# Attention with softcap, then a mixture of attention experts: the spare PSUM bank of the end section becomes a tile of its own

## Chip, cores and metric

One Trainium2 chip, one of its cores. The metric is the device time of one execution in microseconds (us), smaller is better; the time of a kernel is the median of its runs.

## The reference

Eight sequences of 448 tokens. First an attention with 12 heads of 64, whose scores pass through a soft cap of 30; then, on its output as 768 features, four attention experts of head size 64 with causal scores, of which each token uses the two that its gate ranks highest.

```python
scores = cap * np.tanh((q @ k.T) / sqrt(64) / cap)        # 8 x 12 heads, 448 x 448
attn = softmax(scores);  x = (attn @ v) as (8, 448, 768)

logits = x @ w_gate                                        # 4 experts, top 2 by logits
for e in range(4):
    qe, ke, ve = x @ wq[e], x @ wk[e], x @ wv[e]           # 768 -> 64
    a = softmax(causal(qe @ ke.T / 8))
    out += (e is chosen) * gate_weight * (a @ ve @ wo[e])  # 64 -> 768
```

## The kernel before

**The work.** The first attention goes in 48 steps, one for each pair of heads of a sequence. For a pair PE fills a score region in PSUM (L534), ACT takes the tanh out of it (L540, `y`), then the exponential of all seven blocks of the pair (L553; for the last pair in two halves, L548), PE multiplies with v (L565, L570), DVE divides (L581, L582, `xk`), and PE and DVE turn the result into `xT` (L592, L622). When the six pairs of a sequence are done, its experts follow, laid between the pairs of the next sequence: gate and v (L672), q and k (L794), expert scores (L813) and their exponential (L820, `pS`), the causal mask on POOL (L828), the product with v (L848, `pvS`), its scaling on DVE (L860, L862, L866, `o`), a sum on POOL (L874), transposes (L884, `otS`), their copy (L894, `oT`), the product with wo (L901), copies to SBUF (L916) and stores (L925).

**PSUM.** Its eight banks are divided by hand. `NAUX = 3` banks are single tiles of pool `ps_aux`, tags `aux0` to `aux2`. The other five are the score regions of pool `ps_score`, tags `sc0` with three banks and `sc1` with two (`CAPS = (8 - NAUX - 2, 2)`), which the tanh groups use in turn.

**The order.** The class `Sched` is a planner that runs while the program is being written: every piece of work has an engine, a duration, the pieces that it depends on and a due time, and the planner issues the pieces in the order of its own simulated clock. The order of each engine's list is thereby fixed (`manual_schedule`); the framework only adds the waits on semaphores, from which tile an instruction reads or writes. In the planner a bank is a number: 0 to 2 are the aux banks, and number 3 (`NAUX`) is the spare, which becomes free late, when the last tanh has read the three-bank region (`note_t` adds the piece `("spare",)`). A piece that takes bank 3 gets its tile from `spare()` instead of from `ps_aux` (in `Sched.aux`).

**The end section.** For the last sequence nothing is left to lay its experts between, so `add_last` has its own pieces (dictionary `L`). Once the last pair's tanh groups are done, the two score regions are taken as two end tiles (`l_tile`): one of three banks, and one of two. In the three-bank tile, banks 0 and 1 hold first q and k of experts 0 and 1 (L1036, copied to `qL`, `kL` by DVE and ACT, L1043), then the scores of one expert of each pair (L1111, read by ACT in L1117, `pL`), then an output block (L1186). The two-bank tile does the same for experts 2 and 3 and for the other expert of each pair. Bank 2 of the three-bank tile is the spare. Ten pieces pass through it in this execution, all of them named `end` in the profile because they share the tile: pvS of two windows (L848, read by L860 to L866), a pv of the last pair (L565, L570, read by L581, L582), v of two windows (L1050, read by ACT and DVE, L1075), a product with v (L1144, read by L1153 to L1160) and four output blocks (L901, read by L916). The masks of the last sequence are L1126, on POOL for experts 0 and 1 and on DVE for the others; the transposes and their copies are L1166 and L1176.

The order of PE's list from 288.7 us on is: q and k of feature block 4, pvS (spare), the gate, q and k of block 5 for experts 0 and 1, the same for 2 and 3, pvS (aux), v (spare, aux, spare), scores of experts 0 and 1, v (aux), v (spare, aux, spare, aux), pvS (aux), scores of 2 and 3, products with v (spare, aux), and then transposes and output blocks.

Of the kernel before, what the change touches and what calls it, by code (L numbers as in the profile page):

```python
# [9 lines left out]
f32 = mybir.dt.float32  # L10
# [230 lines left out]
def kernel(  # L241
# [37 lines left out]
    xp = ctx.enter_context(tc.tile_pool(name="xp", bufs=2))  # L279
    bp = ctx.enter_context(tc.tile_pool(name="bp", bufs=2))  # L280
    outp = ctx.enter_context(tc.tile_pool(name="outp", bufs=2))
    ps_score = ctx.enter_context(
        tc.tile_pool(name="ps_score", bufs=1, space=bass.MemoryType.PSUM)
    )
    ps_aux = ctx.enter_context(tc.tile_pool(name="ps_aux", bufs=1, space=bass.MemoryType.PSUM))
    CAPS = (8 - NAUX - 2, 2)

    ctx.enter_context(tc.manual_schedule())
# [223 lines left out]
    def group_of(i, cap):  # L512
        s = info[i]
        slots = []
        if s["rem"]:
            c = s["rem"].pop(0)
            slots = [(0, 0, c), (1, 1, c)]
        if s["tail"] and (not slots or (cap == 3 and s["reads"] > 0)):
            slots.append((len(slots), 0, KC))
            s["tail"] = False  # L520
        return slots, not s["rem"] and not s["tail"]

    def a_fill(p, slots, sc, tails):
        qt, kk = qkt[p]
        for at, g, c in slots:
            if (c == KC) != tails:
                continue
            o = sc[:, at, 0:S]
            r = slice(0, 128) if c == KC else slice(64 * g, 64 * g + 64)
            qs = qt[r, :]  # L530
            if p >= FIRST_Q:
                o = o.rearrange("p (m c t) -> p m c t", c=QC, t=16)
                qs = qs.rearrange("p (c m t) -> p m c t", c=QC, t=16)
            nc.tensor.matmul(o, kk[r, 128 * c : 128 * (c + 1)], qs, start=True, stop=True)  # L534
# [481 lines left out]
    L = {}  # L1016

    def l_tile(par):
        par = tail_par[par]
        if ("tile", par) not in L:  # L1020
            L["tile", par] = ps_score.tile(
                [128, CAPS[par], 512], f32, name=f"end{par}", tag=f"sc{par}"
            )
        return L["tile", par]

    def spare():
        x = [x for x in (1, 2) if tail_par[x] == 0][0]
        return l_tile(x)[:, 2, :]

    sch.spare = spare  # L1030

    def l_qk(r, which, j):
        if ("qk", r) not in L:
            L["qk", r] = l_tile(1 - r)
        w2 = wq2 if which == "q" else wk2
        nc.tensor.matmul(  # L1036
            L["qk", r][:, "qk".index(which), 0:S], w2[r][:, j, :], xT[LB][:, j, :],
            start=(j == 0), stop=(j == NDC - 1),
        )
# [64 lines left out]
    def l_fill(r):  # L1104
        ps = [L.setdefault(("s", r, g), l_tile(1 - g)) for g in range(2)]
        for c in (KC, 0, 1, 2):
            k0, q0 = (S - 128, KM) if c == KC else (128 * c, 128 * c)
            o = 0 if c == KC else SCOL[c]
            for g in range(2):
                rr = slice(64 * g, 64 * g + 64)  # L1110
                nc.tensor.matmul(  # L1111
                    ps[g].rearrange("p b c -> p (b c)")[:, o : o + S - q0],
                    kL[r][rr, k0 : k0 + 128], qL[r][rr, q0:S], start=True, stop=True,
                )
# [199 lines left out]
        nc.vector.memset(warm, 0.0)  # L1314

    def c_dummy():
        ps = ps_score.tile([128, CAPS[0], 512], f32, name="dummy", tag="sc0")
        for _ in range(7):
            nc.tensor.matmul(ps[:, 0, :], warm[:, 0:128], warm, start=True, stop=True)

# [70 lines left out]
    add(("warm",), "DVE", 0.27, [], -300.0, c_warm)  # L1391
    add(("ident",), "POOL", 0.6, [], -300.0, lambda: make_identity(nc, ident))
    add(("dummy",), "PE", 3.0, [("warm",)], -300.0, c_dummy)
    add(("table",), "ACT", 1.6, [("warm",), ("ld", "kt1", 0, "issued")], -300.0, c_table)
    for i in range(NST):
# [55 lines left out]
    def next_fill():  # L1451
# [14 lines left out]
        if ("trev", i) not in sch.done:  # L1466
            return None
        r = max(r, sch.done["trev", i][0] + 0.05)
        one = dict(r=r, dur=0.4, armed=armed, special=True, go=lambda s: go_t([i], s))
        if nf < 1 or not info[i]["rem"]:  # L1470
            return one
        nxt = pairs_of(i, 1)
        if nxt is None:
# [3 lines left out]
        two = dict(  # L1477
            r=max(r, r2), dur=0.75, armed=armed and armed2, special=True,
            go=lambda s: go_t([i, nxt[0]], s),
        )  # L1480
        if r2 <= max(r, sch.free["PE"]) + 0.05:
# [3 lines left out]
        return one  # L1485

    def tile_of(par):
        return ps_score.tile(
            [128, CAPS[par], 512], f32, name=f"sc_{state['nf']}", tag=f"sc{par}"
        )  # L1490

# [18 lines left out]
    def go_x(x, s, dur):  # L1510
        b, a = x
        sc = tile_of(state["nf"] % 2)
        s_fill(b, a, sc)
        state["x"].pop(0)
        key = ("X", b, a)
        dur += 0.1 if sch.mode == 64 else 0.0
        sch.mode = 128
        sch.free["PE"] = s + dur
        filled(key, s, dur)
        act_op(key, 0.905, [("f", *key)], lambda: s_exp(b, a, sc))  # L1520
# [4 lines left out]
    def go_t(which, s):  # L1525
        todo = []
        t = s + (0.1 if sch.mode == 128 else 0.0)
        for x, i in enumerate(which):
            par = (state["nf"] + x) % 2
            slots, last = group_of(i, CAPS[par])  # L1530
            sc = ps_score.tile(
                [128, CAPS[par], 512], f32, name=f"sc_{state['nf'] + x}", tag=f"sc{par}"
            )
            todo.append((i, slots, last, sc, par))
        ends = {}
        tails = 0.1
        for tail in (False, True):
            for x, (i, slots, last, sc, par) in enumerate(todo):
                a_fill(i, slots, sc, tail)
                k = sum(1 for at, g, c in slots if (c == KC) == tail)  # L1540
                if tail:
                    if k:
                        t += tails + S / 2400 + 0.003
                        tails = 0.0
                        ends[x] = t
                else:
                    t += k // 2 * (S / 2400 + 0.003)
                    ends[x] = t
        sch.mode = 64 if tails else 128
        sch.free["PE"] = t  # L1550
        for x, (i, slots, last, sc, par) in enumerate(todo):
            note_t(i, slots, last, sc, par, s, ends[x] - s)

    def note_t(i, slots, last, sc, par, s, dur):
        f = info[i]
        first, num = f["nb"], f["reads"]
        for at, g, c in slots:
            f["idx"][g, c] = first + at
        f["nb"] += len(slots)
        f["reads"] += 1  # L1560
        key = ("T", i, num)
        filled(key, s, dur)
        if i == NK - 1:
            tail_par[num] = par
            if par == 0 and num > 0:
                add(("spare",), "-", 0.0, [("T", i, num)], 0.0, lambda: None)
        adur = len(slots) * S / 1200 + 0.055
        act_op(key, adur, [("f", *key)], lambda: a_tanh(i, slots, sc, first))
        if num == 0 and i > 0:
            act_op(  # L1570
                ("E", i - 1), 7 * S / 1200 + 0.095, e_deps(i - 1), lambda: a_exp(i - 1)
            )
        if last:
            sch.finish(("filled", i), s + dur, "PE")
            state["piece"] += 1
            if i == NK - 1:
                for u, n in enumerate((WIN[2], S - WIN[2])):
                    act_op(
                        ("E", i, u), 7 * n / 1200 + 0.095, e_deps(i),
                        lambda u=u: a_exp_half(i, u),  # L1580
                    )
# [43 lines left out]
```

## Time and profile before

| | |
|---|---|
| median of 11 runs | 319.76 us (318.04 to 322.27) |
| the profiled execution | 318.04 us, of which the span of the profile is 316.0 |
| granted TensorE clock, mean | 0.971 |
| busy: PE matmul, PE weight load | 268.6 us (85%), 172.9 (55%) |
| busy: DVE, ACT, POOL | 203.4 (64%), 290.0 (92%), 177.1 (56%) |
| first matmul into an end tile | 282.74 us |
| end of the last exponential of the last pair | 286.44 us |
| last copy to SBUF starts (DVE) | 310.38 us |

Times within the profile count from the start of the span. A row of the timeline gives the start, the time from the start of its first to the end of its last instruction, the engine, the line of the kernel, the operation with what it writes and reads, and how many instructions it merges; in brackets stands the idle time of the engine just before it, and what ended it. A row of busy time by stretch gives for PE, PE weight load, DVE, ACT and POOL the busy time and the count of instructions, then the granted TensorE clock, the busy share of the 16 DMA engines, and the GB/s that they moved.

### The profile page before, as it was taken

The numbers are of one execution on the slowest core, as the hardware profiler recorded it, in microseconds if no ns is written. First come the engines' busy times: TensorE is split into PE (matmuls) and PEld (weight loads), VectorE is DVE, ScalarE is ACT, GpSimd is POOL, SyncE is SP. The second block draws the span as 40 slices with busy tenths as digits, with TensorE's granted clock in tenths as the row PEclk, the third lists the DMA queues.
The fourth block names the chain that finished last, engine by engine and source line by source line (L and its number), as shares of the span: only waits on it lengthen the run. The fifth ranks groups of instructions, "written<-read, shape, count | busy, mean of one in ns | idle before, by whom it ended". The sixth has DMA issues, their size and how long they took to land.

```text
span 316.0 us, 8056 instructions
## 1 busy us (share of the span) xinstructions
PE 268.6 (85%) x3073; PEld 172.9 (55%) x3073; DVE 203.4 (64%) x660; ACT 290.0 (92%) x229; POOL 177.1 (56%) x342
## 2 busy tenths in 40 slices
PE   6677678988899989998899899999899899987681
PEld 2344445665556755566555655755447565655550
DVE  3087435667477686757777566687576767654792
ACT  4889999999999999999999999999999999993541
POOL 6449690899419753678433993983439726230500
PEclk9579999999999999999999999999999999999997
DMA  5999999975988179943999186956899431020027
GB/s 161 266 230 210 235 205 158 212 188 142 227 229 206 37 193 199 308 101 86 205 282 228 23 220 151 259 152 192 225 235 250 97 99 52 2 75 2 0 95 256
DMA packets 93190, 52.87 MB, mean 167 GB/s; under 512 B 53792, under 2 KB 89760, under 8 KB 93152
## 3 DMA queue, kind: packets, MB, share of 16 engines
q1 hardware_dynamic: 81888, 50.19, 64.9%
q0 software_dynamic: 10512, 1.58, 7.2%
q10 hardware_dynamic: 752, 0.59, 0.8%
q8 instruction: 24, 0.39, 0.5%
q14 instruction: 14, 0.11, 0.1%
HBM read 36.19 MB, written 11.01 MB: 149 GB/s over the span
## 4 chain that ended last, share of the span: by engine, by line
ACT 64%; PE 19%; issue 6%; DVE 6%; POOL 3%; DVEq 0%; ACTq 0%; POOLq 0%
ACT pbuf L553 30%; ACT y L540 28%; ACT pS L820 4%; PE sc L534 3%; PE sc L813 2%; PE pv L570 2%; PE vps L672 1%; PE end L1036 1%; PE kps L794 1%; PE pv L565 1%; PE qps L794 1%; POOL ee L734 1%; PE wops L901 1%; DVE qs L803 1%; POOL mb L720 1%
## 5 line engine op out<-in xcount | busy, mean ns | idle before, releaser
L540 ACT ACTIVATE y<-sc 128x896 f16<-128x896 f32 x144 | 144.6, 1137 | 2.9 <-PE sc L534 2.9
L553 ACT ACTIVATE pbuf<-y 128x3136 f16<-128x3136 f16 x47 | 137.3, 2921 | 0.0
L534 PE MATMUL sc<-qk 64*128 64x448 f16 (+1 forms) x336 | 62.3, 367 | 11.6 <-ACT y L540 7.5
L570 PE MATMUL pv<-v,pbuf 128*128 128x65 f16 x1140 | 60.0, 194 | 0.0
L570 PEld LDWEIGHTS <-pbuf 128*128 128x128 f16 x1152 | 52.8, 98 | 4.8 <-issue 1.9
L565 PE MATMUL pv<-v,pbuf 128*128 128x130 f16 x190 | 42.8, 225 | 12.4 <-ACT pbuf L553 9.8
L534 PEld LDWEIGHTS <-qk 64*128 64x128 f16 (+1 forms) x336 | 20.3, 94 | 44.3 <-issue 36.8
L399 POOL CAST q<-qf 112x512 f16<-112x512 f32 x46 | 28.2, 615 | 26.3 <-DMA qf<-in_q_dram 26.0
L582 DVE TENSOR_TENSOR xk<-pv,rc 128x256 f16<-128x256 f32 x95 | 40.3, 425 | 3.3
L720 POOL COPY mb<-mk 128x1024 f16<-128x1024 f16 x14 | 14.2, 1039 | 45.2 <-DVE mk L715 45.2
L409 POOL CAST v<-vst 128x512 f16<-128x512 f32 x48 | 28.3, 619 | 7.4 <-DMA vst<-in_v_dram 7.4
L565 PEld LDWEIGHTS <-pbuf 128*128 128x128 f16 x192 | 18.8, 98 | 24.6 <-ACT pbuf L553 15.2
L581 DVE RECIPROCAL rc<-pv 128x4 f32<-128x4 f32 x95 | 16.9, 178 | 22.1 <-PE pv L570 21.6
L828 POOL TENSOR_TENSOR pS<-pS,keep 128x128 f16<-128x128 f16 (+1 forms) x56 | 21.0, 395 | 15.9 <-ACT pS L820 14.3
L622 DVE COPY xT<-xtp 128x448 f16<-128x448 f16 x48 | 18.5, 387 | 17.6 <-PE xtp L592 17.6
L916 DVE COPY ob<-wops 128x384 f32<-128x384 f32 (+1 forms) x48 | 25.5, 555 | 5.8 <-PE wops L901 5.2
L672 PE MATMUL vps<-wvg,xT 128*128 128x260 f16 x168 | 28.0, 275 | 0.0
L403 POOL CAST k<-kst 128x512 f16<-128x512 f32 x42 | 25.8, 616 | 0.1
L901 PE MATMUL wops<-wo,oT 128*128 128x384 f16 x112 | 24.9, 326 | 0.5 <-DVE o L866 0.2
L734 POOL TENSOR_TENSOR ee<-euler,lg 128x16 f32<-128x16 f32 x7 | 20.4, 2913 | 8.6 <-DVE lg L679 8.6
L794 PE MATMUL kps<-xT,wk 128*128 128x448 f16 x84 | 22.2, 352 | 0.9 <-DVE ob L916 0.4
L794 PE MATMUL qps<-xT,wq 128*128 128x448 f16 x84 | 22.3, 352 | 0.0
(171 smaller groups left out, 425.7 us busy)
## 6 DMA issues: line engine op xcount, KB each, us to landing
qf<-in_q_dram SPq DMA_DIRECT2D x22, 448.0 KB, 5.4
vst<-in_v_dram SPq DMA_DIRECT2D x23, 384.0 KB, 5.1
kst<-in_k_dram SPq DMA_DIRECT2D x22, 384.0 KB, 4.5
out_dram<-ob SPq DMA_DIRECT2D x18, 384.0 KB, 3.0
kst<-in_k_dram SPq DMA_DIRECT2D x47, 32.0 KB, 4.8
vst<-in_v_dram SPq DMA_DIRECT2D x47, 32.0 KB, 4.4
out_dram<-ob SPq DMA_DIRECT2D x6, 192.0 KB, 3.1
out_dram<-vst SPq DMA_DIRECT2D x3, 384.0 KB, 2.3
```

Of the source, the lines that this page charges most:

```text
L399: cp(c16["q", p], src.rearrange("p h (c d) -> p c h d", c=QC))
L403: cp(c16["k", p][:, 0:n], src.rearrange("p h c d -> p c h d")[:, 0:n])
L409: cp(v16[p % NV][:, :, :, 0:Dh], src)
L534: nc.tensor.matmul(o, kk[r, 128 * c : 128 * (c + 1)], qs, start=True, stop=True)
L540: nc.scalar.activation(ytile[i][:, first : first + nb, :], sc[:, 0:nb, 0:S], AF.Tanh, scale=isc / capf)
L553: nc.scalar.activation(ptile[i], ytile.pop(i), AF.Exp, scale=capf)
L565: nc.tensor.matmul(pv[:, n, :, :], ptile[i][:, idx[0, KC], w : w + 128], v16[i % NV][:, :, KC, :], start=(n == 0), stop=False, skip_group_ ...
L570: nc.tensor.matmul(pv[:, n, g, :], ptile[i][:, idx[g, c], w : w + 128], v16[i % NV][:, g, c, :], start=False, stop=(c == KC - 1), skip_gro ...
L582: nc.vector.tensor_tensor(xk, pv[:, :, :, 0:Dh], rc.broadcast_to((128, 2, 2, Dh)), ALU.mult)
L672: nc.tensor.matmul(ps, xT[b][:, j, w : w + 128], wvg[:, j, :], start=(j == 0), stop=(j == NDC - 1),)
L794: nc.tensor.matmul(s[which, r], w2[r][:, j, :], xT[b][:, j, :], start=(j == 0), stop=(j == NDC - 1),)
L901: nc.tensor.matmul(ps, s["oT"][:, r, w : w + 128], wo2[r][:, f * (D // 2) : (f + 1) * (D // 2)], start=(r == 0), stop=(r == 1),)
```

## The change

The pool `ps_score` becomes two pools, one for each region, so that each can be closed by itself. `ps_aux` is opened before them, and the regions lie at the two sides of what is left, so bank numbers change. At the end of the program the pool of a region is closed and a pool of the same size is opened in its place: with one two-bank tile, and, where the region had three banks, with a one-bank tile `spare` beside it. `spare()` hands out that tile instead of bank 2 of the end tile. The pieces, their order on each engine and their operands are as before.

```diff
-    ps_score = ctx.enter_context(
-        tc.tile_pool(name="ps_score", bufs=1, space=bass.MemoryType.PSUM)
-    )
     ps_aux = ctx.enter_context(tc.tile_pool(name="ps_aux", bufs=1, space=bass.MemoryType.PSUM))
+    sides = ("left", "right")
+    ps_ctx = [ctx.enter_context(ExitStack()) for _ in range(2)]
+    ps_score = [
+        ps_ctx[i].enter_context(
+            tc.tile_pool(
+                name=f"ps_score{i}", bufs=1, space=bass.MemoryType.PSUM, side=sides[i]
+            )
+        )
+        for i in range(2)
+    ]
...
     def l_tile(par):
         par = tail_par[par]
         if ("tile", par) not in L:
-            L["tile", par] = ps_score.tile(
-                [128, CAPS[par], 512], f32, name=f"end{par}", tag=f"sc{par}"
-            )
+            ps_ctx[par].close()
+            pool = ctx.enter_context(
+                tc.tile_pool(
+                    name=f"ps_end{par}", bufs=1, space=bass.MemoryType.PSUM, side=sides[par]
+                )
+            )
+            L["tile", par] = pool.tile([128, 2, 512], f32, name=f"end{par}", tag="end")
+            if par == 0:
+                L["spare"] = pool.tile([128, 512], f32, name="spare", tag="spare")
         return L["tile", par]
 
     def spare():
         x = [x for x in (1, 2) if tail_par[x] == 0][0]
-        return l_tile(x)[:, 2, :]
+        l_tile(x)
+        return L["spare"]
...
     def tile_of(par):
-        return ps_score.tile(
+        return ps_score[par].tile(
             [128, CAPS[par], 512], f32, name=f"sc_{state['nf']}", tag=f"sc{par}"
         )
```

The tiles of `c_dummy` and `go_t` are taken from `ps_score[0]` and `ps_score[par]` in the same way.

More of the change, by code (lines that the diff above doesn't have):

```diff
@@ L1316, in c_dummy @@
     def c_dummy():
-        ps = ps_score.tile([128, CAPS[0], 512], f32, name="dummy", tag="sc0")
+        ps = ps_score[0].tile([128, CAPS[0], 512], f32, name="dummy", tag="sc0")
         for _ in range(7):
@@ L1530, in go_t @@
             slots, last = group_of(i, CAPS[par])
-            sc = ps_score.tile(
+            sc = ps_score[par].tile(
                 [128, CAPS[par], 512], f32, name=f"sc_{state['nf'] + x}", tag=f"sc{par}"
```

## The prediction

> **What bounds the kernel now.** I read the page first, then the chain of waits, then the timeline from 281 us by engine, then busy time by stretch of the last 10 us. The page says where the change can act at all.
>
> ```profile
> span 316.0 us, 8056 instructions
> ACT  4889999999999999999999999999999999993541
> ```
>
> ScalarE is full for nine tenths of the span; the change touches nothing there. From slice 37 (284 us on) no engine is full: this is the end section, a chain through PE, DVE, ACT and POOL, and it alone uses the end tiles. The timeline shows what it waits for.
>
> ```profile
> 289.55 0.35 PE L1036 MATMUL end<-xT,wq 128*128 128x448 f16 x1
> 290.95 0.35 PE L1036 MATMUL end<-xT,wk 128*128 128x448 f16 x1 [1.06 <-DVE o L866]
> 292.58 0.49 PE L1050 MATMUL end<-wvg,xT 128*128 128x256 f16 x3 [0.40 <-DVE qL L1043]
> 292.91 0.49 PE L1050 MATMUL lv<-wvg,xT 128*128 128x256 f16 x3
> 295.65 0.49 PE L1050 MATMUL end<-wvg,xT 128*128 128x256 f16 x3 [0.95 <-ACT pL L1117]
> 299.44 0.34 PE L1144 MATMUL end<-vall,pL 128*128 128x65 f16 x6 [1.11 <-ACT pL L1117]
> ...
> 289.93 0.18 DVE L860 RECIPROCAL end<-end 128x2 f32<-128x2 f32 x1 [0.61 <-PE end L1036]
> 293.06 0.17 DVE L860 RECIPROCAL pvS<-pvS 128x2 f32<-128x2 f32 x1
> ...
> 294.30 0.37 ACT L1075 CAST vall<-end 128x256 f16<-128x256 f32 x1 [0.91 <-PE end L1111]
> ```
>
> In each row with a wait, one side works in banks 0 and 1 of the three-bank end tile (L1036, L1043, L1111, L1117) and the other in bank 2, the spare (L860, L866, L1050, L1075, L1144). No value passes between them. L860 needs what L848 wrote (289.11 to 289.61) and waits for a later q matmul; the k matmul needs xT (ready at 289.32) and waits for L866. So the order is kept per tile, not per bank. The two rows without a wait are the control: lv (292.91) and pvS are separate tiles of one pool, and PE writes lv while DVE is about to read pvS.
>
> Then what follows the compute.
>
> ```profile
> 306.00:308.00 2.00, 2.00 (x15) 1.20 (x13) 1.84 (x4) 1.18 (x3) 0.00 (x0) 1.00 0.88 346
> 308.00:309.00 1.00, 1.00 (x7) 0.47 (x5) 0.65 (x2) 0.66 (x2) 0.00 (x0) 1.00 1.01 399
> 312.00:313.00 1.00, 0.00 (x0) 0.00 (x0) 0.00 (x0) 0.00 (x0) 0.00 (x0) 0.50 0.97 252
> ```
>
> The last two columns are DMA share and GB/s: from about 306.2 to 314.1 the stores fill the DMA engines. The end therefore moves with the time at which the first stores come, not with the last DVE copy.
>
> **The change, part by part.** Nothing is added to any engine's list; no DMA is issued anew or moved. Each region is handed over once: the first matmul into it, at 282.74, already waits for the last tanh (0.17 us, from ACT L540), and should still do so. I cost the handover, the new bank numbers and the splitting of one score pool into two at 0; the trace has no row for them. What goes are the waits between the spare and banks 0/1. I follow the lists with the durations of the trace; handing over from engine to engine is 0.03 to 0.05 us there.
>
> 1. Before 286.5: the k matmul at 284.83 waited 0.51 for L866. Gain 0, because the pv matmuls at 286.49 wait for the exp half that ends at 286.44, and PE runs without a gap from there to 289.55.
> 2. The k matmul of 290.95 follows the q matmul by one step of 0.19: 289.74, 1.21 earlier. kL on ACT: 290.13 instead of 291.34. L860 starts at 289.64, after the last pvS matmul, so L866 ends at 290.62 and does not stand before qL. The qL copy still waits for kL (same tile, stays): 290.69. Second qL ends at 291.85 instead of 293.06: gain 1.21.
> 3. pvS moves to 290.31; lv into the spare needs only L866: 290.81 instead of 292.58 (1.77). Three groups of 0.33 fill PE to 291.79; the score matmuls L1111 need qL: about 291.9 instead of 293.66 (1.75).
> 4. ACT: vall no longer waits for L1111 and is done at about 292.5, when the scores are; pL starts at 292.5 instead of 294.57 (2.05). POOL's mask L1126 (3.23) runs 293.7 to 296.95 instead of 295.74 to 298.97 (2.0).
> 5. PE: the second lv into the spare no longer waits for pL: 292.8 instead of 295.65, and the second L1111 at 294.9 instead of 297.72 (2.8). That is more than the path can use, because POOL is now late next: the L1144 group needs the mask, 297.0 instead of 299.44, and POOL's L874 (1.15), which had waited for L866, stands right behind the mask at 296.97 instead of 299.05 (2.05).
> 6. From L874: otS 298.2, oT on ACT 298.85, then two lot copies behind it (0.80, 0.36, 0.36 apart), so the first L1186 at 300.4 instead of 302.50 (2.1). The L1186 group at 303.74 waited 0.30 for the vst copy out of the spare; that wait goes: 301.4 (2.35). The ACT copy of vst, 304.63 at present, follows: 302.3; on DVE the L1153 chain, which stood behind the vst copy, starts 2.45 earlier.
> 7. First stores therefore 2.35 to 2.45 earlier, and the full DMA stretch (7.9 us) moves as a whole. The last DVE copies lose two more waits (ACT kst at 309.32 is one) and end about 3.0 earlier, but hidden behind full DMA engines: 0 more.
>
> Sum: 2.4 us. The profiled execution took 318.04 (span 316.0 and 2.04 around it), so 315.6 with a span of 313.6. It is the fastest of the 11 runs; taking the same 2.4 from the median, 319.76, gives 317.4, a 0.75% gain. A measurement of this kernel tells about 0.5% (1.6 us) from no change.
>
> [...] In the trace wtokL (L1101) took 0.78 while POOL's L874 ran, where a product of the same shape with POOL idle (L1088) took 0.18. [...] With the change wunL and wtokL fall into POOL's mask (mask pieces of 0.42). [...] By the rows POOL's mask steps were evenly 0.38 apart and wunL beside a mask piece took 0.29: sum 2.4. I take the rows and keep 2.0 for the range.
>
> Bounds for what has no row. The handover: 0 if it waits as now; 0.1 if each region waits for both regions' last tanh (ending 283.49, 0.75 after the present one; the 0.51 wait that goes and the exp bound absorb most); above that see the third rival. Bank numbers: 0 either way, the granted clock of 1.00 and the durations of one shape agree across tiles now. If the stores do not bind after all, the gain is 3.0.
>
> **The rivals.** *Partial gain.* [...] Removing only the wait of 290.95 gives 1.0 to 1.2: 318.6.
>
> *No change.* The order might be kept by region or by pool, not by tile, so the split would remove nothing. Against: lv and pvS above. 319.8.
>
> *Slower.* Taking a new region may wait for more than the old region's own readers. If the matmul of 282.74 had to wait for ACT's list up to the last exp half (286.44), the PE work that now lies between 282.74 and 286.49 (3.75 less the 0.51 wait and small gaps of 0.2, so about 3.0) would come after it: 3.0 later at that point. The relief afterwards is 2.4 by the sum above, so 0.6 slower: 320.4. It decides from a handover ending at about 285.8; a loss over 1.6 us needs one up to 287.4, such as a wait for the last xk (288.21: 322.2). Against: the present row names ACT y L540 alone, and the old region's readers are only such tanh and exp reads.
>
> **How the numbers follow.** My forecast (1.8 to 3.0 gained) 0.74, partial 0.12, no change 0.07, slower 0.07. Within the forecast the case runs from 316.8 to 318.0; with about 0.3% for what a median moves between sets of runs (the 11 runs spread from 318.04 to 322.27), 316.2 to 318.5. The partial case reaches to 319.0 with it, so the range is 316.2 to 319.1; no change and slower are left out. Faster by over 0.5%: 0.74. Within 0.5%: the partial case, no change and half of slower with what noise adds, 0.21. Slower by over 0.5%: 0.05.
>
> **What would show it.** Right: the waits of L1036 on L866, of L1050 on qL and pL, of vall on L1111 and of L1144 on pL are gone; kL starts near 290.1, pL near 292.5, the mask near 293.7 and ends near 297, with L874 straight behind it; DMA is full from about 303.8 to 311.7. Wrong: the first matmul into a region starts clearly after 282.74; mask pieces over 0.42 us; DMA engines idle between stores.

## The result, and the profile after

| | before | after |
|---|---|---|
| median | 320.65 us (318.04 to 322.9, 50 runs) | 318.27 us (316.32 to 323.04, 13 runs) |
| ratio after / before | | 0.993, 95% interval 0.9908 to 0.9952 |
| profiled execution | 318.04 us, span 316.0 | 317.33 us, span 315.0 |
| last exponential of the last pair ends | 286.44 | 287.96 |
| from there to the end of the span ("the end") | 29.51 | 27.04 |

The change is faster by 0.7%, some 2.3 us. The two profiled executions differ by less, because everything up to the last exponential came 1.52 us later in the one of after. The profiled execution of before is the fastest of its 50 runs. The kernel below with new pools but no split has the main loop of after, and its runs take 0.9992 of the time of before (0.9969 to 1.0014). So the later start is put down to the execution, not to the change; in the ten other profiled kernels below, which all have that main loop, the last exponential ends anywhere from 287.25 to 293.32. All comparisons of profiles below therefore count from the end of the last exponential; to compare a row of after with one of before, take 1.52 off it. The lines of the kernel have moved by 7 to 14: L1050 was L1036, L1064 was L1050, L1125 was L1111, L1131 was L1117, L1140 was L1126, L1158 was L1144, L881 was L874, L891 was L884.

Two lines of the page of after; the second is ScalarE's busy share in 40 slices of the span.

```profile
span 315.0 us, 8054 instructions
ACT  4989999999999999999999999999999999995641
```

The same picture as before: ScalarE is full until the end section, and only there can anything have moved. These are the rows of the timeline of after that answer to those shown of before.

```profile
284.26 0.35 PE L1050 MATMUL end<-xT,wq 128*128 128x448 f16 x1 [0.17 <-ACT y L547]
...
291.07 0.35 PE L1050 MATMUL end<-xT,wq 128*128 128x448 f16 x1
291.26 0.35 PE L1050 MATMUL end<-xT,wk 128*128 128x448 f16 x1
292.33 0.49 PE L1064 MATMUL spare<-wvg,xT 128*128 128x256 f16 x3
294.29 0.49 PE L1064 MATMUL spare<-wvg,xT 128*128 128x256 f16 x3
296.90 0.20 PE L1158 MATMUL spare<-vall,pL 128*128 128x65 f16 x1
297.35 0.59 PE L1158 MATMUL spare<-vall,pL 128*128 128x65 f16 x5 [0.25 <-POOL pL L1140]
299.73 0.34 PE L891 MATMUL otS<-plain,o 128*128 128x128 f16 x3 [1.02 <-POOL o L881]
...
293.61 0.36 ACT L1089 CAST vall<-spare 128x256 f16<-128x256 f32 x1
294.05 1.94 ACT L1131 ACTIVATE pL<-end 128x1024 f16<-128x1024 f32 x2
...
295.21 3.23 POOL L1140 TENSOR_TENSOR pL<-pL,keep 128x128 f16<-128x128 f16 x8 [9.79 <-ACT pL L1131]
298.52 1.15 POOL L881 TENSOR_TENSOR o<-o 128x512 f16<-128x512 f16 x1
```

The k matmul follows its q matmul by 0.19; its wait of 1.06 for L866 is gone, and so are those of the v matmuls (0.40 and 0.95) and of the copy of `vall` (0.91). Where the products with v had waited 1.11 for ACT's reading of the end tile, they now wait 0.25 for POOL's mask, a real input. POOL's sum (L881) stands straight behind its mask and is what the transposes (L891) wait for: POOL is late next.

Busy time by stretch of after; the last three columns are granted TensorE clock, DMA share and GB/s.

```profile
304.00:305.00 1.00, 0.86 (x7) 0.52 (x7) 1.00 (x4) 0.22 (x2) 0.00 (x0) 1.00 0.00 0
305.00:306.00 1.00, 1.00 (x8) 0.59 (x6) 0.94 (x3) 0.67 (x2) 0.00 (x0) 1.00 0.97 387
312.00:313.00 1.00, 0.00 (x0) 0.00 (x0) 0.00 (x0) 0.00 (x0) 0.00 (x0) 0.90 1.01 326
313.00:314.00 1.00, 0.00 (x0) 0.00 (x0) 0.00 (x0) 0.00 (x0) 0.00 (x0) 0.50 0.19 74
```

The stores fill the DMA engines from 305.0 to about 313.2, for some 8 us as in before, and they begin and end earlier by about what the compute gained. (`vst` and `kst` are the SBUF tiles from which the last output blocks are stored; `otS` and `lot` are the transposed products of the last but one and of the last sequence, `oT` the copies of both.)

### The profile page after: what moved, and what is told of

Read it like the earlier page. It is cut to its first block, busy times and chain, and to the rows that moved or that the text cites. A ratio compares the mean times of both kernels' runs of the same rounds, so it can differ in the third digit from the quotient of the medians.

```text
span 315.0 us, 8054 instructions
## 1 busy us (share of the span) xinstructions
PE 271.2 (86%) x3073; PEld 174.6 (55%) x3073; DVE 203.1 (64%) x660; ACT 290.3 (92%) x229; POOL 177.1 (56%) x342
## 4 chain that ended last, share of the span: by engine, by line
ACT 60%; PE 19%; DMA 6%; issue 6%; DVE 4%; POOL 4%; POOLq 0%; ACTq 0%; DVEq 0%; SPq 0%
ACT pbuf L560 27%; ACT y L547 27%; ACT pS L827 5%; PE sc L541 4%; DMA qf<-in_q_dram 3%; DMA kst<-in_k_dram 2%; PE pv L577 2%; PE sc L820 2%; PE pv L572 1%; PE vps L679 1%; PE kps L801 1%; PE end L1050 1%; POOL ee L741 1%; PE wops L908 1%; PE qps L801 1%
## 5 line engine op out<-in xcount | busy, mean ns | idle before, releaser
L547 ACT ACTIVATE y<-sc 128x896 f16<-128x896 f32 x144 | 143.9, 1120 | 3.7 <-PE sc L541 3.7
L541 PE MATMUL sc<-qk 64*128 64x448 f16 (+1 forms) x336 | 63.7, 375 | 10.6 <-ACT y L547 6.8
L577 PE MATMUL pv<-v,pbuf 128*128 128x65 f16 x1140 | 60.9, 196 | 0.0
L577 PEld LDWEIGHTS <-pbuf 128*128 128x128 f16 x1152 | 53.8, 99 | 5.2 <-issue 2.4
L727 POOL COPY mb<-mk 128x1024 f16<-128x1024 f16 x14 | 14.2, 1039 | 45.0 <-DVE mk L722 45.0
L572 PEld LDWEIGHTS <-pbuf 128*128 128x128 f16 x192 | 19.1, 99 | 21.8 <-ACT pbuf L560 11.6
```

Of the source, the lines that this page charges most:

```text
L547: nc.scalar.activation(ytile[i][:, first : first + nb, :], sc[:, 0:nb, 0:S], AF.Tanh, scale=isc / capf)
L572: nc.tensor.matmul(pv[:, n, :, :], ptile[i][:, idx[0, KC], w : w + 128], v16[i % NV][:, :, KC, :], start=(n == 0), stop=False, skip_group_ ...
L577: nc.tensor.matmul(pv[:, n, g, :], ptile[i][:, idx[g, c], w : w + 128], v16[i % NV][:, g, c, :], start=False, stop=(c == KC - 1), skip_gro ...
```

## The experiments

Times are us after the end of the last exponential, from one profiled execution of each kernel; "end" is the end of the span. The theory was that the gain is the sum of what each removed wait costs at its place, and that new pools, new bank numbers and the handover of a region bring and cost nothing. The rivals: the pools or the banks themselves are the gain; a wait is worth more or less than its place says; or something later than the waits sets the end.

| kernel | k copy (kL) | pL | mask | transposes (otS) | first store | last DVE copy | end |
|---|---|---|---|---|---|---|---|
| before | 4.90 | 8.13 | 9.31 | 13.82 | 18.70 | 23.94 | 29.51 |
| after | 3.69 | 6.09 | 7.25 | 11.76 | 16.22 | 20.84 | 27.04 |
| new pools, not split | 4.91 | 8.14 | 9.31 | 13.82 | 18.69 | 23.93 | 29.54 |
| last two waits back | 3.69 | 6.09 | 7.25 | 11.76 | 16.22 | 21.44 | 27.06 |
| first two waits back | 4.92 | 7.32 | 8.49 | 13.00 | 18.61 | 22.85 | 29.20 |
| the same, again | 4.92 | 7.32 | 8.49 | 13.00 | 18.71 | 22.94 | 29.32 |
| the same, with filling | 4.92 | 7.32 | 8.49 | 13.01 | 17.46 | 22.07 | 28.38 |
| middle three waits back | 3.69 | 6.94 | 8.12 | 12.63 | 18.63 | 23.07 | 29.38 |
| the same, again | 3.69 | 6.94 | 8.12 | 12.62 | 18.57 | 22.81 | 29.14 |
| the same, with filling | 3.69 | 6.95 | 8.12 | 12.64 | 17.22 | 22.14 | 28.34 |

**New pools without the split.** The regions are closed and opened anew as in after, but the three-bank region is one tile again and the spare its bank 2.

```diff
-            L["tile", par] = pool.tile([128, 2, 512], f32, name=f"end{par}", tag="end")
-            if par == 0:
-                L["spare"] = pool.tile([128, 512], f32, name="spare", tag="spare")
+            L["tile", par] = pool.tile([128, CAPS[par], 512], f32, name=f"end{par}", tag="end")
...
-        l_tile(x)
-        return L["spare"]
+        return l_tile(x)[:, 2, :]
```

> The pools are closed and opened as in the changed kernel, with the new bank numbers, but the three-bank region is one tile again and the spare is its bank 2. Measure: time from the end of the last exponential half of the last pair to the end of the span, 29.6 us before (286.44 to 316.0), 27.0 in the changed kernel (287.96 to 315.0). Theory (the order is kept per tile, the split is the whole gain, the handover costs nothing): 29.6 again, all six waits between spare and end back, ratio to before 0.998 to 1.002. Rival (the handover or the other banks bring the gain): 27.0, ratio 0.993. Rival (the handover itself costs and the split gains more than it seems): over 29.8.

Measured: ratio to before 0.9992 (0.9969 to 1.0014), end 29.54, every step within 0.01 to 0.03 of before. Its timeline has the four waits of PE again, to the hundredth:

```profile
294.22 0.35 PE L1047 MATMUL end<-xT,wk 128*128 128x448 f16 x1 [1.06 <-DVE o L873]
295.85 0.49 PE L1061 MATMUL end<-wvg,xT 128*128 128x256 f16 x3 [0.40 <-DVE qL L1054]
298.92 0.49 PE L1061 MATMUL end<-wvg,xT 128*128 128x256 f16 x3 [0.95 <-ACT pL L1128]
302.71 0.34 PE L1155 MATMUL end<-vall,pL 128*128 128x65 f16 x6 [1.11 <-ACT pL L1128]
```

So the handover and the bank numbers are worth nothing that shows (0.03 us of the end), and the split is the whole of the gain. It also settles the slower rival: that mechanism would show here as a loss with nothing beside it.

**The last two waits put back.** The copy of an output block out of the end tile waits again for a later output matmul into the spare, and the copy out of the spare for a copy out of the end tile (`after` adds such an order between two instructions).

```diff
+        if (b, n, f) == (LB, 3, 0):
+            after(i, ("wo", LB - 1, 2, 0))
+        if (b, n, f) == (LB - 1, 2, 0):
+            after(i, ("ev", LB, 3, 1))
```

> The changed kernel with two of the old waits of the last copies put back: the kst copy of the last rows waits for the output matmul into the spare, the vst copy out of the spare waits for the ACT kst copy. Theory (the stores fill the DMA engines and set the end): the last DVE copy starts 0.6 later against the exp end, the span end does not move (27.0, within 0.15). Rival (the last copies set the end): 27.6.

Measured: the last DVE copy 0.60 later, the end 27.06 against 27.04. The waits that the change takes from the last copies are worth nothing: the DMA engines cover them, full with a busy share of 1.01 from 309.79 to 313.20 here.

**The first two waits put back.** The k matmul waits again for L873 out of the spare, and L867 of that window for the last q matmul.

```diff
+        if (b, n) == (LB - 1, 1):
+            after(i, "wq")
...
+        if (r, which, j) == (0, "k", NDC - 1):
+            after(i, ("o", LB - 1, 1))
```

> The changed kernel with two of the old waits put back: the k matmul of the last feature block waits for L873 reading the spare, and L867 before it waits for the q matmul. Theory (steps add up along one chain): the k matmul comes 1.2 us later against the exp end, the second score fill and the mask follow, and the exp end to span end takes 28.2 (27.0 plus 1.2). Rival (everything hangs on this first wait): 29.5. Rival (POOL's mask or the stores set the end anyway): 27.0 to 27.3.

Measured: kL, mask and the transposes 1.23 to 1.24 later, as expected, but the end at 29.20: 2.16 lost instead of 1.2. Up to the transposes the theory holds; behind them another 1 us goes that no wait accounts for.

**The middle three waits put back.** The first v matmul into the spare waits for qL, the copy of `vall` for the score matmuls, the second v matmul into the spare for the first pL.

```diff
+            if (n, j) == (0, 0):
+                after(m, ("q", 0))
+            if (n, j) == (2, 0):
+                after(m, ("x", 0, 0))
...
+            if n == 0:
+                after(i, ("f", 0))
```

> The changed kernel with three of the old waits put back: v into the spare waits for the first qL copy, the vall copy waits for the first score fill, the third v group waits for the first pL. Theory: the fill comes 0.4 later, the second fill 1.5 later, of which POOL's mask path hides 0.3; exp end to span end 28.2 (27.0 plus 1.2). Rival (everything hangs on the first wait): 27.0. Rival (each wait counts by its own idle time, 0.40, 0.91 and 0.95): 29.3.

Measured: mask and transposes 0.87 later, the end at 29.38: again 2.34 lost where 1.2 was expected. Either group alone put back thus takes away nearly the whole gain, which two separate costs cannot do. The busy time by stretch shows what the extra is, in a column that I had not counted with: the granted clock stands at 0.50 for 3.4 us, from 14.1 us after the last exponential in the first kernel and from 14.9 in the second. In before and after it is 1.00 from there to the last matmul.

**Both again, with runs for a ratio.** The mean granted clock differs from run to run (0.945 to 0.987 over the 55 runs of before beside these two), so both kernels ran once more.

> The two first waits put back once more (the k matmul behind the softmax work on the spare bank, and the first sum of sequence 6 behind the last q matmul), because in the first look TensorE's granted clock was 0.50 for some 3 us of the end and its length could not be used. Theory (every put-back wait moves the whole end by what it costs at its place): mask start 8.49 us after the last exponential (7.25 in the changed kernel), first sum of the last sequence otherwise as there, first store 17.45, end 28.2 us after the last exponential where the clock holds 1.00; ratio to the kernel before 0.997. Rival (the slow stretch belongs to the put-back wait): the clock is at 0.50 again at the same place, and the end comes at 29.2.

> The three middle waits put back once more, for the same reason. Theory: mask start 8.12 us after the last exponential, second filling of the spare bank 10.11, first store 17.1 to 17.45, end 27.9 to 28.2 where the clock holds 1.00; ratio to the kernel before 0.996 to 0.997. Rival (the slow stretch belongs to the waits): the clock at 0.50 again, end at 29.4.

Measured: ratios 1.0004 (0.9981 to 1.0028) and 1.0000 (0.9970 to 1.0031), ends 29.32 and 29.14, the clock at 0.50 again from 14.2 on in both. Three rows of the second of them, in the columns of the stretches above:

```profile
302.00:303.00 1.00, 1.00 (x6) 0.36 (x4) 0.92 (x6) 0.34 (x2) 0.00 (x0) 0.50 0.00 0
303.00:304.00 1.00, 1.00 (x17) 0.83 (x16) 0.76 (x3) 0.00 (x0) 0.00 (x0) 0.50 0.00 0
304.00:305.00 1.00, 1.00 (x13) 0.65 (x10) 0.89 (x5) 0.00 (x0) 0.00 (x0) 0.50 0.03 8
```

PE is full there. Two of the 384-column output matmuls (302.55) take 0.84 us from start to end, and 0.50 in after. So it is no chance: all four profiles of these two kernels show it, and their other runs lose the whole gain too.

**The waits put back, and PE kept at work.** In the four profiles with the fall PE has matmuls under way for only 1.67 to 2.06 us of the 3.41 before it, and waits there for POOL's sum (1.03 in the second profile with the first two waits back, 1.02 in both with the middle three). My guess was that too little work is the cause; then work without use in that wait must cure it:

```diff
         ps = sch.aux(("oT", b), [128, 2, 512], f16, f"otS_{b}")
+        if b == LB - 1:
+            for _ in range(14):
+                nc.tensor.transpose(ps[:, 0, 0:128], plain, plain)
```

> The two first waits put back, and 14 more 128-column transposes of a constant on TensorE ahead of the last sequence-6 transposes, into the tile that these overwrite: about 0.8 us of TensorE work that lies in its wait for the sum of that sequence. Theory (the half clock of the two earlier profiles comes from too little TensorE work in the stretch before it, not from the waits as such): granted clock 1.00 through the end, transposes at 13.0 us after the last exponential as without the filling, first store 17.45, end 28.2 to 28.3; ratio to the kernel before 0.996. Rival (the clock has another cause): 0.50 again at about 14.2 after the last exponential, end 29.2 to 29.3, ratio 1.000.

> The three middle waits put back, with the same filling. Theory: granted clock 1.00 through the end, transposes at 12.6 us after the last exponential, first store 17.1 to 17.3, end 27.9 to 28.2; ratio to the kernel before 0.995 to 0.996. Rival: 0.50 again from 14.1 to 14.9 on, end 29.1 to 29.4, ratio 1.000.

Measured: ends 28.38 and 28.34, each about 0.1 above the range expected, ratios 0.9964 (0.9936 to 0.9991) and 0.9959 (0.9927 to 0.9990). Against the ratios without filling the intervals still overlap a little, so the weight lies on the profiles, one of each kernel. Two rows of the timeline and one stretch of the first of them:

```profile
299.64 0.95 PE L893 MATMUL otS<-plain 128*128 128x128 f16 x14
300.84 0.34 PE L896 MATMUL otS<-plain,o 128*128 128x128 f16 x3 [0.24 <-POOL o L883]
```

```profile
303.00:304.00 1.00, 1.00 (x23) 0.87 (x24) 0.78 (x3) 0.00 (x0) 0.00 (x0) 1.00 0.00 0
```

The filling lies in the wait for L883, of which 0.24 is left, and the transposes start where they did. The clock stays at 1.00 up to the last matmul, and 0.94 and 0.80 us of the end come back, counted from the second profiles without filling. Now the waits cost what lies at their place: the first two 28.38 - 27.04 = 1.34, the middle three 1.30. Their sum, 2.64, is near the whole gain of 2.47.

**One sum moved from POOL to DVE.** Since POOL is late next, its sum for the last but one sequence is taken by VectorE right behind the last product of that sequence (in `s_pvev`); and in a second kernel POOL, free then, takes the mask of expert 2.

```diff
+        s["no"] = s.get("no", 0) + 1
+        if b == LB - 1 and s["no"] == 4:
+            o = s["o"]
+            nc.vector.tensor_tensor(
+                o[:, :, 1:5:3, :], o[:, :, 1:4:2, :], o[:, :, 2:5:2, :], ALU.add
+            )
...
     def s_oa(b):
+        if b == LB - 1:
+            return
```

The second kernel has this line besides:

```diff
-            (nc.vector if r else nc.gpsimd).tensor_tensor(
+            (nc.vector if 2 * r + g == 3 else nc.gpsimd).tensor_tensor(
```

> The changed kernel with the one sum of sequence 6 that stands between its products and its transposes (GpSimd, 1.15 us behind a 3.23 us mask) taken by VectorE right after the last product. Theory (with the waits gone GpSimd's mask and sum set the path to the transposes): the transposes start about 1.0 us earlier than 11.76 after the last exponential, VectorE's chain behind them is later by 0.3 to 0.45, the first output product starts 0.5 earlier, the end comes at 26.5 (27.04 in the changed kernel); ratio to the kernel before 0.9915. Rival (VectorE is itself full there, 293.4 to 301.3 without a gap, and takes back what GpSimd gives): the end at 27.0 or later, ratio 0.993 or above.

> The same, and the mask of expert 2 (0.72 us of VectorE) taken by GpSimd, which has nothing else to do there. Theory: the first output product as in the version with the sum alone, the second group of products over the last sequence is not held up by VectorE, end at 26.4; ratio to the kernel before 0.991. Rival (two SBUF inputs on VectorE beside GpSimd slow each other): small VectorE rows of 0.16 us stretch to 0.3 or more, end at 26.8 or later.

Measured: the sum alone gives 317.49 us, ratio 0.9904 (0.9868 to 0.9939), end 26.81; with the mask moved as well 317.92 us, 0.9919 (0.9897 to 0.9941), end 26.94. The first is the fastest of all kernels here by median and by end, but its interval overlaps that of after. From the timeline of the first:

```profile
295.39 3.42 POOL L1148 TENSOR_TENSOR pL<-pL,keep 128x128 f16<-128x128 f16 x8 [9.78 <-ACT pL L1139]
...
297.64 0.50 DVE L881 TENSOR_TENSOR o<-o 128x512 f16<-128x512 f16 x1
298.90 0.17 DVE L1123 TENSOR_TENSOR wtokL<-wunL,rdenL 128x16 f32<-128x16 f32 x1
...
299.89 0.28 PE L1188 MATMUL lot<-plain,oscL 128*128 128x128 f16 x2 [0.38 <-DVE oscL L1182]
300.65 0.23 PE L1188 MATMUL lot<-plain,oscL 128*128 128x128 f16 x1 [0.47 <-DVE oscL L1182]
```

The transposes start at 10.77 instead of 11.76, and the first output matmul at 12.64 instead of 13.38. But PE now waits for `oscL`, the products of the last sequence that DVE scales, and DVE, which has no gap there, comes to the output copies later: the first store gains 0.66, the second only 0.36, and the end 0.23 of the 0.5 expected. The rival of a full DVE holds for half. In the second kernel the end of 26.4 did not come either: as its rival said, the row of `wtokL` stretched (to 0.44, against 0.17 with POOL idle), the first output matmul came 0.26 after that of the first kernel, and the end is at 26.94.

## Why the prediction was right

**The map.** The forecast was a gain of 0.75%, 317.4 us, within 316.2 to 319.1; 0.7% and 318.27 came. Over 50 runs the median of before is 320.65, 0.89 above the 319.76 of 11 runs on which the forecast stood, which is the 0.87 that the figure in us missed by. The margin for that was thinner than stated: the range goes 0.5 to 0.6 us beyond the forecast's 316.8 to 318.0, while the 0.3% named for it would be almost 1 us. The times of the working, moved by the 1.52 of this execution, against the rows of after:

| step | forecast | after |
|---|---|---|
| 1 first matmul into an end tile waits as before | 0.17 for L540 | 0.17 for L547 |
| 2 k matmul; kL | 291.26; 291.65 | 291.26; 291.65 |
| 3 v into the spare; scores | 292.33; 293.4 | 292.33; 293.40 |
| 4 pL; mask | 294.0; 295.2 | 294.05; 295.21 |
| 5 second v into the spare; second scores; sum L881 | 294.3; 296.4; 298.5 | 294.29; 296.36; 298.52 |
| 6 transposes; oT; last-sequence output group; vst copy | 299.7; 300.4; 302.9; 303.8 | 299.73; 300.38; 302.78; 303.68 |
| 7 first store; last DVE copy; end | -2.35 to -2.45; -3.0; -2.4 | -2.48; -3.10; -2.47 |

The rows of the table hold to 0.15 us. That the 2.4 was not the sum of the removed waits (1.06 + 0.40 + 0.95 + 1.11 alone is 3.5) came from step 5, where POOL takes over as what is late, and from step 7, where full DMA engines cover the rest. The last-two-waits run shows step 7, and POOL's row (L881, 1.02 of PE's wait) step 5. Two terms were off. The `lot` copies behind `oT` took 0.60 for both, where the 0.73 of before was counted, and steps 6 and 7 came 0.1 earlier for it. And the products with v were put at 297.0 (298.5 here), behind the whole mask, but the first started at 296.90 and the rest from 297.35 on, each when the mask pieces that it needs were done. That moved nothing, since the sum on POOL ends later.

**DVE beside POOL.** The range kept a gain of 2.0 beside the 2.4 of the rows, 0.4 less for DVE and POOL slowing each other. No run shows that term; 2.47 came. DVE rows that are longer beside POOL are there, but they are small; the first two are of before, the third is of after:

```profile
299.05 1.15 POOL L874 TENSOR_TENSOR o<-o 128x512 f16<-128x512 f16 x1
299.45 0.78 DVE L1101 TENSOR_TENSOR wtokL<-wunL,rdenL 128x16 f32<-128x16 f32 x1
...
298.16 0.32 DVE L1115 TENSOR_TENSOR wtokL<-wunL,rdenL 128x16 f32<-128x16 f32 x1
```

`wtokL` (a product of gate weights, both inputs in SBUF) takes 0.32 beside POOL's mask pieces in after, 0.44 beside them in the kernel with the mask moved, 0.17 with POOL idle, and had taken 0.78 in before, beside POOL's long sum: it ended when that sum did. So the change made this row shorter, not longer. `wunL`, the product before it, went from 0.29 to 0.36, and POOL's mask took 3.23 as before, so POOL lost nothing beside the two. In the kernel with the sum on DVE it did: beside DVE's 0.50 of L881 the mask took 3.42, 0.19 longer.

**The rivals.** No change by tile: refuted by the split against the unsplit pools. Slower through the handover: refuted by the 0.17 of the first matmul and by the unsplit pools. Partial gain: only in the sense of step 5, where POOL is late next, and that was in the sum.

**What the prediction had not seen.** It argued that gains of separate waits add up along the path. Here that held with the clock at 1.00 only. A change that had taken away only one of the two groups of waits is worth 1.1 us with the clock held (29.51 less 28.38 or 28.34), and measured as nothing. The partial rival's 1.0 to 1.2 for the first wait alone is wrong for the same reason: with the middle three waits back, so that the first two (and the last two) stay removed, the ratio is 1.0000. And that after keeps its clock was taken for granted, not worked out. By the kernels that fell, about 1 us of the gain hung on it, and so far the hit is luck.

## What to carry to other kernels

When two parts of one PSUM tile are used for unrelated work, look for waits for a value that the waiting instruction doesn't read: here four of PE's, of 1.06, 0.40, 0.95 and 1.11 us. Giving the parts tiles of their own removed them without moving an instruction. The gain was found by following the lists to the next late engine and to the stores (2.4 forecast, 2.47 measured), not by adding up the waits (3.5). And where waits change what PE does for some 3 us, read the granted clock behind that stretch before and after: in this end section, waits of 1.34 and 1.30 us cost another 0.94 and 0.80 with the clock at 0.50, and work without use on PE in a wait gave that back.

## What the runs showed of the hardware that was not expected

TensorE's granted clock fell here with PE at work. In the four profiles with the first two or the middle three waits put back, and no filling, it fell to 0.50 for 3.4 us although PE had matmuls under way for 1.67 to 2.06 us of the 3.41 us before. The busy share does not tell these from the kernels that kept the clock: before has 2.08 in its like stretch, after 2.06, and the kernel with the last two waits back 1.74.

```profile
297.89:301.30 3.41, 2.06 (x31) 1.46 (x31) 3.12 (x17) 1.97 (x3) 2.14 (x4) 1.00 0.00 0
```

That is the stretch ahead of the fall in the first run with the first two waits back. In the nine profiles whose clock was read over a longer part, the falls to 0.50 within an execution lie whole multiples of 3.41 us apart (in after at 9.02, 22.63, 36.32, 43.15 and 312.90, which are 4, 8, 10 and 89 steps behind the first). The like stretch is the step, counted back from a later fall, that ends between 13.6 and 15.0 us after the last exponential. Eleven of the twelve profiles show such a fall and have that step; in those that fell it ends at 14.1 to 14.9, so its place does not sort the cases.

The columns that the matmuls streamed in the like stretch, each matmul counted by the share of its time inside, are about 2,700 and 2,500 in the second profiles of the two kernels that fell, and about 3,700 in after and 4,500 each in before and in the first kernel with filling, which kept the clock. Earlier in the program they do not sort the cases: in after the 3.41 us from 5.61 to 9.02, with about 4,300 columns and PE at work for 2.03 us, were followed by 0.50, and in the first kernel with filling those from 39.11 to 42.52, with PE at work for 1.75, were too. What sets the clock is thus not shown by these runs, beyond that the filling kept it at 1.00 in the two kernels that had lost it. Whether some of the other runs of after fell was not tried.
